# Exponentials on VectorE in int16, four tiles at once, and background matmuls as column tiles

## The chip, the core and the metric

The kernel runs on one core of a Trainium2 chip, as one launch. The metric is the device time of one execution in microseconds. Five engines work in parallel, each through its own queue of instructions in order: PE (TensorE, matmuls), ACT (ScalarE), DVE (VectorE), POOL (GpSimd) and SP, which here only issues DMAs. Matmuls write to PSUM, which here is eight banks of 128 x 512 fp32.

## The reference

One input x of 2048 rows and 512 columns (bf16) is normalised by rows, and the result goes through attention with 32 heads of 16 and through a gated feed-forward block; the output is x plus both.

```
xn = _layernorm(x)
# attention: q, k, v of 32 heads, 16 wide each
scores = jnp.einsum("bhqd,bhkd->bhqk", q, k) * (Dh ** -0.5)
p = _softmax(scores, axis=-1)
o = jnp.einsum("bhqk,bhkd->bhqd", p, v)
# feed-forward: F = 1792
gate = jnp.einsum("bsd,df->bsf", xn, W_gate);  up = jnp.einsum("bsd,df->bsf", xn, W_up)
h = gate * (gate > 0) * up
return x + o_as_rows @ wo + jnp.einsum("bsf,fd->bsd", h, W_down)
```

The softmax needs 32 x 2048 x 2048 exponentials. They are the bulk of the elementwise work.

## The kernel before

**Tiles of scores.** The heads stand eight to a group of 128 partitions (four groups, gg), two to each 32 partitions (ee is 0 or 1, j is 0 to 3). A tile is one head, 128 keys and 512 queries, so that there are 2048 tiles in the order c4 (512 queries), gg, ee, kt (128 keys), j. A score matmul contracts over 32 partitions, in which the other of the two heads is masked to zero; the mask is on k: `proj_k` writes two copies of kT, one for each ee (line 561), and `proj_q` one of qT (line 551; the first one on ACT, line 549). The four j use four row groups of the array (`tile_position=(32 * j, 0)`, line 796), and can run at the same time.

**Exponentials.** ACT takes the tiles in units of 3 and 2 in turn, out of two sets of score banks (ps_sc: three and two banks), and writes bf16 to a ring of 7 slots for each size (line 865). 208 tiles, spread evenly over tiles 96 to 2007, go to DVE in pairs (`dve_exp`): a score goes to bank 2 of ps_b (line 796), is scaled and clamped to a fixed-point int32 in dt_sb (line 810, d1), and when two are there, four more instructions of 1024 elements form the exponential of the pair: d2 (line 821), d3 (823), d4 (825) and d5 (828), the last writing the bf16 bit pattern as int16. They read the upper or lower half of each 32-bit word.

**P V.** For each kt, four matmuls (j = 0 to 3) with 17 columns of v_aug (16 of v and one of ones, for the row sum) stand on four column groups of the array and accumulate in bank 0 of ps_b over the 16 kt of a block (line 777). After each of the 32 blocks (c4, gg, ee), `normalise` copies the bank out (line 749), brings the sums through three DMAs and a reciprocal to all partitions, and POOL multiplies (line 764).

**Background.** The projections, the feed-forward block (`glu`: 56 pieces with eight matmuls, a copy of up, line 649, and a gate product, line 653, each; weights by two DMAs a piece) and the output rows (`out_rows`) run beside the attention. All of them go through `mm_chain` (line 537): full 128 x 128 matmuls in groups of two, with bank 1 of ps_b as the target, and a wanted place for each group among the units of ACT (`slots`; at most one group to a unit). Where a unit has no such work, the score group begins with a matmul on zeros (line 848), whose output the scores then overwrite.

**What sets the order.** Nothing is scheduled on the chip: the program builds a list of operations (`G.op`), each with an engine, a duration in ns as the writer puts it, a priority and the tiles that it reads and writes. `Graph.run` plays them through one by one, always placing the operation that can start first (by priority among those that are not late), and so fixes each engine's order. Pools with a fixed number of slots (ring, ps_b, ps_sc, ws, hT and so on) add waits for a slot's last users. `emit` then puts in the semaphore waits. So a change of any duration or priority can reorder everything.

Of the kernel before, what the change touches and what calls it, by code (L numbers as in the profile page):

```python
# [28 lines left out]
NRING = 7  # L29
PV_LAG = 7.0  # L30
NWS = 3
NDR = 3
ND_TILES = 210
D_FIRST = 96
D_LAST = 2048 - 40
# [3 lines left out]
C_K = 0.07802452  # L39
C_C = 1.83833913  # L40
C_A = 1.05904682
C_B = 6.97125146
FX = 65536.0
NUP = 1
NHT = 1
# [20 lines left out]
class Op:  # L66
    __slots__ = ("eng", "dur", "fn", "deps", "order", "prio", "acq", "name", "idx", "start", "end",
                 "done", "left", "users", "signal", "sem", "val", "waits", "stream", "lat", "seq", "hb", "after")


class Graph:
# [4 lines left out]
    LAT = {"PE": 150.0, "ACT": 220.0, "DVE": 100.0, "POOL": 120.0, "SP": 0.0}  # L76

    def __init__(self):
        self.ops = []
        self.units = {}  # L80

    def op(self, eng, dur, fn, reads=(), writes=(), prio=0.0, order=(), name="", stream=None, lat=None, after=None):
        o = Op()
        o.eng, o.dur, o.fn, o.prio, o.name = eng, dur, fn, prio, name
# [11 lines left out]
        for t in writes:  # L96
            if t.pool is not None and not t.w:
                o.acq.append(t)
            for w in t.w:
                if w.eng == eng and eng == "PE":  # L100
                    o.order.add(w)
                else:
                    o.deps[w] = True
            for r in t.r:
                if r.eng == eng and eng in ("PE", "ACT"):
                    o.order.add(r)
                else:
                    o.deps[r] = True
        for t in reads:
            t.r.append(o)  # L110
# [7 lines left out]
    def run(self):  # L118
# [33 lines left out]
        def earliest(o):  # L152
# [5 lines left out]
            for t in o.acq:  # L158
                b = slot_for(t)
                if b is None:  # L160
                    return None
                at = max(at, b[0])
            return at

        while n < len(ops):
            best = None
            for e in self.ENGS:
                pick = None
                for o in cand[e]:
                    at = earliest(o)  # L170
                    if at is None:
                        continue
                    at = max(at, free[e])
                    late = at > free[e] + 1e-6
                    key = (late, at if late else 0.0, o.prio, o.idx)
                    if pick is None or key < pick[0]:
                        pick = (key, at, o)
                if pick is not None and (best is None or pick[1] < best[0]):
                    best = (pick[1], e, pick[2])
# [4 lines left out]
            for t in o.acq:  # L184
                i = slot_for(t)[1]
# [14 lines left out]
            free[e] = at + o.dur  # L200
# [6 lines left out]
        self.span = max(o.end for o in ops)  # L207

# [102 lines left out]
def bass_parallel_sum__mha_block__glu_gated_reglu__prompt_kernel(  # L311
# [14 lines left out]
    with ExitStack() as es:  # L326
# [23 lines left out]
        kT = sb("kT", [128, 8, S], BF16)  # L350
        qT = sb("qT", [128, 4, 512], BF16)
        v_aug = sb("v_aug", [128, NT, H, VW], BF16)
        ring = sb("ring", [128, NRING * 5, 512], BF16)
        dt_sb = sb("dt_sb", [128, 2, 2 * 512], I32)
        dq_sb = sb("dq_sb", [128, 2 * 512], FP32)
        dw_sb = sb("dw_sb", [128, 2 * 512], BF16)
        dring = sb("dring", [128, NDR, 2 * 512], BF16)
        hT = sb("hT", [128, NHT * FT, 512], BF16)
# [14 lines left out]
        P_dt, P_dv, P_dq, P_dw, P_dr = (Pool(n, k) for n, k in (("dt", 2), ("dv", 1), ("dq", 1), ("dw", 1), ("dr", NDR)))  # L373
# [4 lines left out]
        P_h = Pool("h", NHT)  # L378
# [15 lines left out]
        G.op("DVE", 100, lambda e: e.tensor_scalar(hmask[:, 1:2], pid[:, 0:1], 1.0 / 16.0, None, op0=ALU.mult),  # L394
             reads=[t_pid], writes=[t_mask], prio=-889)
        G.op("DVE", 100, lambda e: e.tensor_scalar(hmask[:, 0:1], pid[:, 0:1], -1.0 / 16.0, 1.0, op0=ALU.mult, op1=ALU.add),
# [63 lines left out]
        def ln_block(b, pr):  # L460
# [11 lines left out]
            for i in range(4):  # L472
                m = 4 * b + i
                t_st, t_mv = Tile(), Tile()
                G.op("DVE", 640, lambda e, m=m: e.bn_stats(stats[:, m, :], xs(m)), reads=[t_xm[m]], writes=[t_st], prio=pr)
                G.op("DVE", 130, lambda e, m=m: e.bn_aggr(mv[:, m, :], stats[:, m, :]), reads=[t_st], writes=[t_mv], prio=pr - 0.1)
# [8 lines left out]
            for i in range(4):  # L485
                m = 4 * b + i
                t_n = Tile("xn", P_xn)
                G.op("DVE", 360, lambda e, m=m, t=t_n: e.tensor_scalar(  # L488
# [5 lines left out]
                elif i % 2 == 0:  # L494
                    tp = Tile("tp", P_b, [0, 1, 2] if b < 3 else [1, 2])
# [19 lines left out]
                elif half == 1:  # L515
# [4 lines left out]
                    o = G.op("DVE", 690, ev, reads=[tp], writes=[Tile()], prio=pr + 0.1)  # L520
# [3 lines left out]
        t_q, t_k, t_v = {}, {}, {}  # L524
# [4 lines left out]
        def mm_chain(tile, pairs, reads, prio, per=2, sub=0, slots=None, dur=220):  # L529

            n = len(pairs)
            for k, a in enumerate(range(0, n, per)):
                def fn(e, a=a):
                    ins = None
                    for i in range(a, min(a + per, n)):
                        l, r = pairs[i]
                        ins = e.matmul(bank_of(tile, sub), l(), r(), start=(i == 0), stop=(i == n - 1))  # L537
                    return ins
                G.op("PE", dur * (min(a + per, n) - a) + 100, fn, reads=reads, writes=[tile],
                     prio=prio if prio < 0 else slots[k] if slots else prio, after=slots[k] if slots else None)  # L540

        def proj_q(c4, gg, prio=0.0, tile=None, sub=0, eng="DVE", slots=None):
# [4 lines left out]
            tq = t_q[(c4, gg)] = Tile("q", P_q)  # L547
            if eng == "ACT":
                G.op("ACT", 600, lambda e: e.activation(qT[:, tq.slot, :], bank_of(t, sub), ACTF.Copy), reads=[t], writes=[tq], prio=prio)
            else:  # L550
                G.op("DVE", 690, lambda e: e.tensor_copy(qT[:, tq.slot, :], bank_of(t, sub)), reads=[t], writes=[tq], prio=prio)

        def proj_k(gg, b, prio=0.0, tile=None, sub=0, slots=None, gap=0.02):
            t = tile or Tile("pk", P_b, [0, 1, 2] if (gg, b) in ((0, 1), (0, 2)) else [1, 2] if gg == 0 else [1])
# [3 lines left out]
            dsts = [kT[:, 2 * gg + ee, 512 * b:512 * b + 512] for ee in range(2)]  # L558
            for ee in range(2):
                tk = t_k[(gg, ee, b)] = Tile("k")  # L560
                G.op("DVE", 690, lambda e, ee=ee: e.tensor_scalar(dsts[ee], bank_of(t, sub), hmask[:, ee:ee + 1], None, op0=ALU.mult),
                     reads=[t, t_masks[ee]], writes=[tk], prio=prio + gap * ee)

        def proj_v(kt, prio, allowed=(1,)):
            t = Tile("pv", P_b, list(allowed))
            mm_chain(t, [((lambda dt=dt: xnT[:, dt, 128 * kt:128 * kt + 128]), (lambda dt=dt: Wv[:, dt, :]))
                         for dt in range(DT)], [t_wv, t_xnT[kt // 4]], prio, slots=[1.3 * kt] * 2)
            tv = t_v[kt] = Tile("v")
            G.op("DVE", 690, lambda e: e.tensor_copy(v_aug[:, kt, :, 0:DH], bank_of(t).rearrange("p (h d) -> p h d", h=H)),  # L569
                 reads=[t], writes=[tv], prio=prio)  # L570
# [4 lines left out]
        on_dve, acc = set(), 0.0  # L575
        for i in range(D_FIRST, D_LAST):
            acc += ND_TILES / (D_LAST - D_FIRST)
            if acc >= 1.0:
                acc -= 1.0
                on_dve.add(i)  # L580
        if len(on_dve) % 2:
            on_dve.discard(max(on_dve))
        units, starts, at_unit, cur = [], [], [], []
        for i, t in enumerate(tiles):
# [4 lines left out]
            if len(cur) == SIZES[len(units) % 2] or i == len(tiles) - 1:  # L589
                units.append(cur)  # L590
                cur = []
        NU = len(units)
# [22 lines left out]
        for kt in range(NT):  # L615
            proj_v(kt, -684 + 10 * (kt // 4) + 0.1 * kt, allowed=(0, 1, 2) if kt < 8 else (1, 2))


        guard = Tile("wv")
        guard.r.extend(t_wv.w + t_wv.r)  # L620
        P_dv.cur[0] = guard
# [12 lines left out]
        def glu(c4, ft, slots):  # L634
            if c4 not in t_h:
# [275 lines left out]
```

## Time and profile before

| | us |
|---|---|
| time, median of 3 runs (904.47 to 912.19) | 908.67 |
| span of the profiled execution, first to last instruction | 901.3 |
| its own time beside the span | not given |
| PE busy, 5328 matmuls | 794.2 |
| DVE busy, 947 instructions | 741.8 |
| ACT busy, 743 instructions | 845.9 |
| POOL busy, 56 instructions | 62.7 |
| mean granted PE clock | 0.976 |

A page of the profile gives each engine's busy time, and busy time counts an instruction from its start to the end of its pipeline, so neighbours overlap; what one instruction costs its engine is the distance from its start to the next start. "Idle before" is put down to the instruction that ended the wait. Line numbers are those of this kernel.

### The profile page before, as it was taken

What the parts mean: (1) busy time and instruction counts of PE and PEld (TensorE: products, weight loads), DVE (VectorE), ACT (ScalarE), POOL (GpSimd) and SP (SyncE); (2) the same over time, 40 slices, a digit from 0 to 9 for tenths busy, and PEclk for the clock granted to TensorE, in tenths of its full rate; (3) what the DMA queues carried; (4) which work ended last, traced back from release to release, by engine and by line L of the source; (5) the groups of instructions that cost most, each with busy time, mean ns of one, the idle gap of its engine ahead of it and who ended that gap; (6) DMA issues with size and microseconds to landing.
All of it is one profiled execution on the core that took longest, in us unless ns stands there. A gap on an engine that the chain in (4) does not pass through costs nothing.

```text
span 901.3 us, 13005 instructions
## 1 busy us (share of the span) xinstructions
PE 794.2 (88%) x5328; PEld 220.4 (24%) x5427; DVE 741.8 (82%) x947; ACT 845.9 (94%) x743; POOL 62.7 (7%) x56
## 2 busy tenths in 40 slices
PE   7898898888889998888889999888888999999982
PEld 2322222222222222222222222222222222222220
DVE  8858899999985989979894899989997599999221
ACT  4699999999989999999999999999999999999992
POOL 3200000000000010000000001000000000000000
PEclk9999999999979999999999999999999999999996
DMA  5311111110001121111000011111100122220001
GB/s 172 98 25 37 36 36 37 36 31 19 2 25 36 32 60 35 26 42 48 13 25 25 24 43 48 43 48 24 25 13 25 36 54 60 59 51 16 25 13 36
DMA packets 84091, 34.66 MB, mean 38 GB/s; under 512 B 69952, under 2 KB 79936, under 8 KB 84032
## 3 DMA queue, kind: packets, MB, share of 16 engines
q1 hardware_dynamic: 84032, 33.83, 14.2%
q8 instruction: 42, 0.69, 0.3%
q14 instruction: 17, 0.14, 0.0%
HBM read 31.20 MB, written 2.36 MB: 37 GB/s over the span
## 4 chain that ended last, share of the span: by engine, by line
ACT 56%; PE 30%; DVE 8%; DMA 2%; issue 1%; POOL 0%; SPq 0%; POOLq 0%; ACTq 0%
ACT ring L865 56%; PE ps_b L537 11%; PE ps_sc L796 9%; PE ps_b L777 5%; PE ps_sc L848 3%; PE ps_b L796 2%; DVE dq_sb L823 2%; DMA rb<-rec_scr 1%; DVE dt_sb L810 1%; DVE Wv L821 1%; DVE xn_sb L488 1%; DVE dw_sb L825 1%; DMA x_sb<-in_A_x_dram 1%; DVE dring L828 1%; DVE v_aug L569 0%
## 5 line engine op out<-in xcount | busy, mean ns | idle before, releaser
L865 ACT ACTIVATE ring<-ps_sc 128x1536 bf16<-128x1536 f32 x736 | 841.5, 1270 | 29.0 <-PE ps_sc L796 26.8
L796 PE MATMUL ps_sc<-qT,kT 32*128 32x512 bf16 x1840 | 291.8, 388 | 43.9 <-ACT ring L865 36.2
L777 PE MATMUL ps_b<-ring,v_aug 128*17 128x512 bf16 x1840 | 192.4, 385 | 3.5 <-DVE o_sb L749 1.5
L810 DVE TENSOR_SCALAR dt_sb<-ps_b 128x512 int32<-128x512 f32 x208 | 142.1, 683 | 20.9 <-PE ps_b L796 16.1
L828 DVE SCALAR_TENSOR_TENSOR dring<-dt_sb,dw_sb 128x1024 int16<-128x1024 int16 x104 | 129.3, 1243 | 9.5 <-PE ps_b L777 9.3
L796 PEld LDWEIGHTS ps_sc<-qT,kT 32*128 32x128 bf16 x1840 | 70.3, 91 | 258.5 <-ACT ring L865 163.9
L823 DVE SCALAR_TENSOR_TENSOR dq_sb<-dt_sb 128x1024 f32<-128x1024 uint16 x104 | 130.6, 1255 | 0.0
L825 DVE SCALAR_TENSOR_TENSOR dw_sb<-dq_sb,Wv 128x1024 bf16<-128x1024 f32 x104 | 128.9, 1239 | 0.3
L848 PE MATMUL ps_sc<-zeros 128*128 128x512 bf16 x235 | 90.9, 387 | 17.7 <-ACT ring L865 16.8
L764 POOL TENSOR_TENSOR x_sb<-o_sb,rb 128x512 bf16<-128x512 f32 x28 | 43.1, 1540 | 695.6 <-DMA rb<-rec_scr 628.7
L796 PE MATMUL ps_b<-qT,kT 32*128 32x512 bf16 x208 | 80.3, 386 | 3.2 <-DVE dt_sb L810 1.8
L777 PE MATMUL ps_b<-dring,v_aug 128*17 128x512 bf16 x208 | 80.1, 385 | 0.0
L777 PEld LDWEIGHTS ps_b<-ring,v_aug 128*17 128x17 bf16 x1840 | 45.4, 88 | 126.2 <-issue 118.1
L821 DVE TENSOR_SCALAR Wv<-dt_sb 128x1024 f32<-128x1024 uint16 x104 | 72.2, 694 | 1.5
L537 PE MATMUL ps_b<-Wd,hT 128*128 128x512 bf16 x209 | 65.8, 402 | 3.9 <-issue 2.6
L537 PE MATMUL ps_b<-xnT,wgs 128*128 128x512 bf16 x216 | 61.5, 383 | 4.2 <-DVE up_sb L649 2.8
L537 PE MATMUL ps_b<-xnT,wus 128*128 128x512 bf16 x197 | 61.1, 390 | 4.4 <-issue 4.1
L653 DVE SCALAR_TENSOR_TENSOR hT<-ps_b,up_sb 128x512 bf16<-128x512 f32 x56 | 38.4, 686 | 12.8 <-PE ps_b L537 12.3
L848 PEld LDWEIGHTS ps_sc<-zeros 128*128 128x128 bf16 x261 | 25.1, 96 | 86.5 <-ACT ring L865 70.9
L649 DVE COPY up_sb<-ps_b 128x512 f32<-128x512 f32 x56 | 38.3, 684 | 5.1 <-PE ps_b L537 4.8
L749 DVE COPY o_sb<-ps_b 128x512 f32<-128x512 f32 x32 | 22.0, 688 | 15.8 <-PE ps_b L777 15.7
L537 PE MATMUL ps_b<-Wo_p,x_sb 128*128 128x512 bf16 x101 | 31.9, 386 | 1.6 <-issue 1.1
(60 smaller groups left out, 300.5 us busy)
## 6 DMA issues: line engine op xcount, KB each, us to landing
rb<-rec_scr SPq DMA_DIRECT2D x32, 256.0 KB
wus<-in_B_W_up_dram SPq DMA_DIRECT2D x56, 128.0 KB, 2.5
wgs<-in_B_W_gate_dram SPq DMA_DIRECT2D x56, 128.0 KB, 2.3
xr_sb<-in_A_x_dram SPq DMA_DIRECT2D x16, 128.0 KB, 4.1
out_dram<-xn_sb SPq DMA_DIRECT2D x16, 128.0 KB, 1.7
Wd<-in_B_W_down_dram SPq DMA_DIRECT2D x1, 1792.0 KB, 8.5
x_sb<-in_A_x_dram SPq DMA_DIRECT2D x3, 512.0 KB, 4.2
Wv<-in_A_wqkv_dram SPq DMA_DIRECT2D x1, 512.0 KB, 6.0
```

The source lines that it names most:

```text
L537: ins = e.matmul(bank_of(tile, sub), l(), r(), start=(i == 0), stop=(i == n - 1))
L653: G.op("DVE", 690, lambda e: e.scalar_tensor_tensor(out=hT[:, FT * th.slot + ft, :], in0=bank_of(tg), scalar=0.0, in1=up_sb[:, tup.slot, : ...
L764: G.op("POOL", 1200, lambda e: e.tensor_tensor(oT_of(tn), o_sb[:, to.slot, :], rb[:, trb.slot, :], ALU.mult), reads=[to, trb], writes=[tn] ...
L777: ins = e.matmul(ps_b[32 * j:32 * j + VN, 0, :], v_aug[:, kt, 8 * gg + 2 * j + ee, 0:VN], src[j][1](), start=(kt == 0), stop=(kt == NT - 1 ...
L796: return e.matmul(bank, kT[32 * j:32 * j + 32, 2 * gg + ee, 128 * kt:128 * kt + 128], qT[32 * j:32 * j + 32, t_q[(c4, gg)].slot, :], start ...
L810: G.op("DVE", 700, lambda e: e.tensor_scalar(dt_sb[:, td.slot, 512 * i:512 * i + 512], ps_b[:, 2, :], 0.25 * LOG2E * FX, -127.0 * FX, op0= ...
L821: G.op("DVE", 600, lambda e: e.tensor_scalar(Wv[:, :, :].rearrange("p a b -> p (a b)").bitcast(FP32), half(0), C_C * FX, C_K / FX ** 3, op ...
L823: G.op("DVE", 1140, lambda e: e.scalar_tensor_tensor(out=dq_sb[:], in0=half(0), scalar=C_A * FX, in1=half(0), op0=ALU.add, op1=ALU.mult), ...
L825: G.op("DVE", 1140, lambda e: e.scalar_tensor_tensor(out=dw_sb[:], in0=dq_sb[:], scalar=C_B * FX * FX, in1=Wv[:, :, :].rearrange("p a b -> ...
L828: G.op("DVE", 1140, lambda e: e.scalar_tensor_tensor(out=dring[:, tr.slot, :].bitcast(I16), in0=half(1), scalar=128.0, in1=dw_sb[:].bitcas ...
L848: e.matmul(ps_sc[:, 3 * k0, :], zeros[:, 0:128], zeros[:], start=True, stop=True)
L865: return e.activation(ring[:, a:a + n, :], ps_sc[:, 3 * k0:3 * k0 + n, :], ACTF.Exp, scale=0.25)
```

## The change

DVE takes 436 tiles and not 208: for each block (c4, gg, ee), the list QUADS says how many of its 16 kt go to DVE whole, with all four j (109 in all). The units of ACT hold the rest.

A quad (`quad`) is four score matmuls through the same bank 2 of ps_b, each followed by one DVE instruction that adds a constant, clamps at zero and writes int16 (d1); then three instructions over all 2048 elements: d2 keeps the lower seven bits and sets an exponent, d3 multiplies that, read as bf16, with the first number, read as bf16, and d4 keeps the exponent bits of the first number. The exponential is the sum of the two bf16 tensors, and is not formed: P V runs twice, once with each (`pv_stream`), and the row sums with it. Three quad buffers stand in place of the fixed-point ones.

The scale that turns a score into an exponent is put into q: `hmask` holds QSCALE and zero, `proj_q` writes two masked copies of qT, and `proj_k` one plain copy of kT. ACT's exp gets a scale to match.

`mm_chain` issues each 128 x 128 matmul as four matmuls of 32 columns on the four column groups, one such four to an operation and not two. Transposes stay as they were.

The planner knows three modes of the array (row tiles, column tiles, full) and charges a change between them; it may start a score on free row groups beside one that has just started; it marks ACT's scores as urgent; it puts a P V on zeros (17 columns, adding nothing) into P V's bank where PE has room, in place of the matmul on zeros before the scores. All durations are written anew. The feed-forward buffer has 20 slots of one piece (hT) and not one of 14, so that the next 512 rows can start before the last are read, and the pieces are spread evenly over the run. The ring has 6 slots of each size. The projections of k, q and v get other wanted places, and the evictions of q, k, v and of the feed-forward block higher priorities.

```diff
 SIZES = (3, 2)
-NRING = 7
+NRING = 6
-NDR = 3
-ND_TILES = 210
-D_FIRST = 96
-D_LAST = 2048 - 40
+NQD = 3
+LEAD = 9
+QUADS = [1] + [3, 4, 3] + [4, 3, 4, 3] * 7
+NHS = 20
...
-                        ins = e.matmul(bank_of(tile, sub), l(), r(), start=(i == 0), stop=(i == n - 1))
+                        w, x = l(), r()
+                        for j in range(4):
+                            ins = e.matmul(bank_of(tile, sub)[32 * j:32 * j + 32, :], w[:, 32 * j:32 * j + 32], x,
+                                           start=(i == 0), stop=(i == n - 1), tile_position=(0, 32 * j))
...
-                G.op("DVE", 690, lambda e: e.tensor_copy(qT[:, tq.slot, :], bank_of(t, sub)), reads=[t], writes=[tq], prio=prio)
+                    G.op("DVE", 655, lambda e, ee=ee: e.tensor_scalar(qT[:, tq.slot, ee, :], bank_of(t, sub), hmask[:, ee:ee + 1], None, op0=ALU.mult),
...
-                G.op("DVE", 690, lambda e, ee=ee: e.tensor_scalar(dsts[ee], bank_of(t, sub), hmask[:, ee:ee + 1], None, op0=ALU.mult),
+            G.op("DVE", 601, lambda e: e.tensor_copy(kT[:, gg, 512 * b:512 * b + 512], bank_of(t, sub)), reads=[t], writes=[tk], prio=min(prio, -600))
...
+        def quad(key, kt, u):
+            c4, gg, ee = key
+            tq = Tile("qd", P_qd)
+            ti, tu = Tile("qi"), Tile("qu")
+            for n, j in enumerate(range(4)):
+                ts = Tile("ds", P_b, [2])
+                t = key + (kt, j)
+                o = G.op("PE", 213, lambda e, t=t: score(e, ps_b[:, 2, :], t), reads=[t_q[key], t_k[(gg, kt // 4)]], writes=[ts],
+                         prio=u - 50, name="dsc", mode="row", rows=[j], after=u - LEAD)
+                G.op("DVE", 601, lambda e, j=j: e.tensor_scalar(qd[:, tq.slot, 0, 512 * j:512 * j + 512], ps_b[:, 2, :], IBIAS, 0.0,
+                                                                op0=ALU.add, op1=ALU.max), reads=[ts], joins=[tq], prio=-500, name="d1")
+                ti.w.append(G.ops[-1])
...
+            G.op("DVE", 600, lambda e: e.tensor_scalar(xu(), xi(), 0x7F, 0x3F00, op0=ALU.bitwise_and, op1=ALU.bitwise_or),
+                 reads=[ti], writes=[tu], prio=u, name="d2")
+            o = G.op("DVE", 1133, lambda e: e.tensor_tensor(xu().bitcast(BF16), xi().bitcast(BF16), xu().bitcast(BF16), ALU.mult),
+                     reads=[ti], writes=[tu], prio=u, name="d3")
...
+            G.op("DVE", 600, lambda e: e.tensor_scalar(xi(), xi(), 0x7F80, 0x0001, op0=ALU.bitwise_and, op1=ALU.bitwise_or),
+                 reads=[ti], writes=[te], prio=u, name="d4")
+            for half, tr in ((1, tu), (0, te)):
+                pv_stream(key, kt, [(lambda j=j, half=half: qd[:, tq.slot, half, 512 * j:512 * j + 512].bitcast(BF16)) for j in range(4)],
+                          [tr, tq], u, u + PV_LAG)
...
-            def sc(e, cl=cl, k0=k0, idle=u > 24 and u not in busy):
+            def sc(e, cl=cl, k0=k0):
                 ins = None
-                if idle:
-
-                    e.matmul(ps_sc[:, 3 * k0, :], zeros[:, 0:128], zeros[:], start=True, stop=True)
...
+        def blank(e):
+            ins = None
+            for j in range(4):
+                ins = e.matmul(ps_b[32 * j:32 * j + VN, 0, :], zeros[:, 0:VN], zeros[:], start=False, stop=False, tile_position=(0, 32 * j))
+            return ins
+        G.filler = (P_b, blank)
```

## Prediction

> **What bounds the kernel now.** I read the page's busy shares first, then the groups by shape, the stages, the longest pieces of the chain of waits, and stretches of the timeline for the real cost of one instruction.
>
> ```profile
> PE 794.2 (88%) x5328; PEld 220.4 (24%) x5427; DVE 741.8 (82%) x947; ACT 845.9 (94%) x743; POOL 62.7 (7%) x56
> ```
>
> ACT is busy for 845.9 us of 901.3 and nearly all of it is the 736 exps of line 865. The stages (us of the stage, then busy us and count of PE, PEld, DVE, ACT, POOL, the granted PE clock, DMA share, GB/s) say where it is not:
>
> ```profile
> 0.00:30.00 30.00, 24.27 (x134) 9.37 (x136) 25.73 (x59) 18.04 (x19) 8.59 (x21) 0.94 0.60 181
> 30.00:60.00 30.00, 26.68 (x182) 8.53 (x185) 22.97 (x35) 21.07 (x19) 4.73 (x3) 0.94 0.06 21
> 100.00:200.00 100.00, 88.23 (x605) 24.92 (x618) 96.22 (x121) 98.35 (x87) 4.58 (x4) 1.00 0.12 29
> 500.00:600.00 100.00, 92.00 (x617) 24.56 (x627) 93.84 (x116) 97.84 (x86) 6.08 (x3) 0.97 0.15 37
> 860.00:901.00 41.00, 21.94 (x138) 5.71 (x138) 7.08 (x11) 23.43 (x21) 2.53 (x2) 0.80 0.08 27
> ```
>
> From 100 us on ACT is full to within 2 or 3%; it loses 21 us in the first 60 us (the first exp starts at 15.9) and 17.6 us behind the last exp. The chain of waits has one unbroken piece that prices an exp: 75.04/66 = 1.137 us for the mean of a 3-tile and a 2-tile exp.
>
> ```profile
> 686.84 75.04 ACT ring L865 x66
> ```
>
> Who waits for whom:
>
> ```profile
> PEld ps_sc L796 <- ACT ring L865: 163.9, 357, 1.2
> ACT ring L865 <- PE ps_sc L796: 26.8, 43, 3.6
> ```
>
> PE waits for ACT to free score banks far oftener than ACT waits for scores. So ACT is the bound; PE and DVE have slack.
>
> Busy PE and DVE are counted with pipeline ends, so I price them from start to start. PE:
>
> ```profile
> 505.45 1.04 PE L537 MATMUL ps_b<-Wd,hT 128*128 128x512 bf16 x4
> 506.42 0.40 PE L777 MATMUL ps_b<-ring,v_aug 128*17 128x512 bf16 x4
> 506.75 0.39 PE L796 MATMUL ps_sc<-qT,kT 32*128 32x512 bf16 x3
> 507.07 0.61 PE L537 MATMUL ps_b<-Wo_p,x_sb 128*128 128x512 bf16 x2
> ```
>
> Three scores on different row groups cost 0.32 us (506.75 to 507.07), a P V group of four column tiles 0.33, four full matmuls 0.97: that is 0.213 to 0.216 for each slot of the array and 0.107 for a change between row tiles, column tiles and the full array. DVE:
>
> ```profile
> 26.89 1.37 DVE L488 TENSOR_SCALAR xn_sb<-x_sb,mv,rstd 128x512 bf16<-128x512 bf16 x4
> 28.18 0.68 DVE L569 CAST v_aug<-ps_b 128x512 bf16<-128x512 f32 x1
> 28.81 0.69 DVE L519 COPY xnT<-ps_b 128x1024 bf16<-128x1024 bf16 x1
> 29.42 0.68 DVE L569 CAST v_aug<-ps_b 128x512 bf16<-128x512 f32 x1
> 32.02 1.38 DVE L561 TENSOR_SCALAR kT<-ps_b,hmask 128x512 bf16<-128x512 f32 x2
> 33.32 0.17 DVE L476 BATCH_NORM_AGGREGATE mv<-stats 128x2 f32<-128x6 f32 x1
> 86.09 0.69 DVE L810 TENSOR_SCALAR dt_sb<-ps_b 128x512 int32<-128x512 f32 x1
> 86.69 1.22 DVE L828 SCALAR_TENSOR_TENSOR dring<-dt_sb,dw_sb 128x1024 int16<-128x1024 int16 x1
> 87.83 0.25 DVE L757 RECIPROCAL rrec<-rsum 128x16 f32<-128x16 f32 x1
> ```
>
> 512 elements from PSUM take 0.60 (86.09 to 86.69), 1024 unpacked ones 1.13 (86.69 to 87.83): 1.035 ns an element and 0.07 fixed. 1024 packed bf16 take 0.61 (28.81 to 29.42): two elements a step. A per-partition mask costs 0.05 more (1.30/2 = 0.65, line 561). The four of line 488 take 1.29, 0.32 each; less 0.07 and two pointers at 0.05 that is 0.15 for 512, between three and four elements a step.
>
> **The change, part by part.**
>
> *ACT.* Tiles on DVE go from 208 to 436 (109 quads of four by the list QUADS), so exps from 736 to 645: 91 x 1.137 = 103.5 us off the engine that bounds. 901.3 - 103.5 = 797.8 if every idle stretch stays as it is. The second ACT copy of q in the prologue, at the 0.60 of the present one (line 549), stands ahead of the first exp: +0.6. The exp's other scale costs nothing.
>
> *DVE.* It loses the old chain, 208 x 0.60 + 104 x (0.60 + 3 x 1.13) = 541. It gains 436 first steps at 0.60 (262) and per quad two bitwise steps and a product of 2048 elements. Bitwise: 0.60 at four a step, 1.13 at two; I take 0.60, since line 488 is the only 16-bit SBUF-to-SBUF row and it lies nearer four. The product reads two packed tensors; no row has that. Its ends are 0.60 and the 2.19 of an unpacked element (line 828's rate); I take 1.13, two a step, because packing gave line 519 two on one input and a second input costs nothing in the 0.60 of the other evictions. Quad: 4 x 0.60 + 2.33 = 4.74; 109 of them 516. K evictions fall from 32 x 0.65 to 16 x 0.60 (-11), q's go from 15 x 0.60 to 30 x 0.65 (+10). The rest (up, hT, O, v, layernorm, sums) stays at about 135. Sum: 706 before, 681 after. Of 764 us between the first exp and the last (797.8 less 16 and 17.6) that is 89%, against 81% now: it still lies beside ACT, but with half the cover.
>
> The Trainium skill ("VectorE: DVE Perf Modes", the perf-mode tier table) gives a 16-bit tensor_scalar from SBUF the 4x mode and tensor_tensor 2x at most; by it the DVE sum is the same 681, and no run here has shown either on int16.
>
> *PE.* Counted along its order of instructions, before and after: slots of the array for the background 992 and 992 (now four 32-column tiles each), P V 512 and 621 (1612/4 = 403 for the tiles of ACT, two for each of 109 quads), idle fillers 261 full ones and 69 column ones; scores 1840 + 208 and 1612 + 436; changes of mode 1803 and 1291. Row time rises from 190 to 199 (same-row neighbours run one behind the other), column time from 111 to 363, full-array time falls from 278 to 7, changes from 193 to 138. Sum: 771 before, 707 after, 93% of 764 where it was 89% of 868. But 56 us of the old sum were fillers with their switches on top, and only 15 of the new are: the part that can't yield rises from about 78% to 90%. That a column tile 32 wide costs what one 17 wide does is not in the trace; its ends are 0.216 a group (506.42) and four times that, and I take 0.216, since these rows differ only in width.
>
> ```profile
> 311.31 0.61 PE L777 MATMUL ps_b<-ring,v_aug 128*17 128x512 bf16 x8
> 312.28 0.39 PE L796 MATMUL ps_sc<-qT,kT 32*128 32x512 bf16 x3
> ```
>
> Sixteen column tiles (four groups, this row and its neighbours) take 0.97 with a switch, again 0.216 a group.
>
> The Trainium skill ("TensorE: Matmul & The Clock Gate", Part 3, measured speedup) speaks against this change: it has 2.38x for three column tiles and 3.07x for four row tiles. By 3.07 a group would cost 0.281, 1682 groups 110 us more, and PE would need 817 us and end the run near 858. The row says 0.216, and the row decides here.
>
> *Waits that are added.* The four scores of a quad pass through one bank (ps_b 2), each behind the DVE step before it. PE is in order, so a late DVE step holds the score of the next exp behind it, and ACT waits. DVE queues up the same way behind its 32 reciprocals, which wait for a DMA (11.3 us in all now, 1.9 at most) and are covered today by 19% of DVE idle. Against it: background work now goes in pieces of 0.216 and not 0.432, so less stands ahead of a due score. ACT's losses between 100 and 860 us are 16 us now. Below, they vanish (-16). Above, PE keeps today's idle share of 11%: 707/0.89 = 794 where ACT alone would take 764 (+30). I take +10, nearer the present rows than either end.
>
> *The rest.* DMAs are the same in number and size; the order of weights among the 32 normalisation chains on SP shifts, and these chains are late-insensitive (POOL stands idle 629 us for them). POOL's instructions are unchanged. The feed-forward block's hT buffer of 20 tiles lets its pieces be spread evenly; the P V ring holds 12 exps and not 14, 13.6 us of ACT, and costs nothing while P V runs less than that behind; if PE falls back further, ACT waits and the PE rival below holds. The tail of 17.6 is the last normalisation chain and stays.
>
> Sum: 797.8 + 0.6 + 10 = 808.4 of span. The page gives no time of this execution beside its span; I add the difference between span and median, 908.67 - 901.3 = 7.4 (the fastest run would make it 3.2). Predicted 815.8, say 816.
>
> **Rivals.** *PE becomes the bound.* For it: 93% of the stretch, and a stall of DVE reaches PE at once. Against it: PE waited 164 us for ACT in its loads alone. From 708 us of PE at today's idle share: 764 -> 794, which ends at 836; with clock dips (0.94 to 0.97 in the stages above) at 850.
>
> *One DVE step is slower than taken.* Bitwise at two a step adds 109 x 2 x 0.53 = 116, the product unpacked adds 109 x 1.06 = 116: DVE 797, which with 16.5 ahead, 17.6 behind and 7.4 makes 838, and 855 with some idle.
>
> *Slower than before.* All three 2048-element steps run unpacked, as every int16 row of the present chain does (line 828). Place: DVE; price: 3 x 2.19 = 6.57 instead of 2.33 a quad, DVE 681 + 462 = 1143, time about 1184. It decides from the point where DVE fills the present time: (867 - 164 - 262)/109 = 4.05 us for the three steps. Against it: line 828's source steps over every second 16-bit word, the new ones are contiguous, like line 488.
>
> *It is all hidden.* Waits shrink with the small pieces and nothing is added: 790 to 799.
>
> **How the numbers follow.** Forecast (own range 800 to 832) 0.63; all hidden 0.12; PE bound 0.12; one slow DVE step 0.07; all slow 0.06. The range 789 to 855 leaves out the last and the fringes. A difference of under 1% can't be told from none here. Faster by over 1%: 0.92; within 1%: 0.02; slower: 0.06.
>
> **What would show it.** Right: 645 exps with unbroken pieces at 1.137; d2 and d4 at 0.60 start to start, d3 at 1.13; ACT's idle between 100 us and the last exp under 35 us; ACT busy at 93%, DVE near 90%. Wrong: start to start of d3 at 2.19 or of d2 at 1.13; four column tiles of the background at more than 0.22; ACT waiting for ps_sc by over 60 us; a granted clock under 0.95 in the middle stages.

## The result and the profile after

The changed kernel takes 797.18 us (median of five runs, 796.42 to 804.70) where the kernel before took 908.67: the ratio is 0.8795, 95% interval 0.8751 to 0.8839. The forecast of 816 had the sign and the range right and is 19 us too high. The execution that was profiled is the slowest of the five: 804.7 us, of which 802.9 are its span. The four others have spans of 794.6 to 796.2, and in every run of this kernel 1.8 us lie around the span.

First the busy shares on the page of the kernel after, and the costliest groups (busy us, mean ns of one, then the idle time before them and what ended it):

```profile
PE 753.1 (94%) x8854; PEld 224.8 (28%) x8854; DVE 717.0 (89%) x1085; ACT 738.0 (92%) x653; POOL 56.5 (7%) x56
...
L965 ACT ACTIVATE ring<-ps_sc 128x1536 bf16<-128x1536 f32 (+1 forms) x645 | 732.9, 1347 | 36.2 <-PE ps_b L883 17.6
L913 DVE TENSOR_SCALAR qd<-ps_b 128x512 int16<-128x512 f32 x436 | 298.3, 684 | 51.1 <-PE ps_b L900 42.4
...
L924 DVE TENSOR_TENSOR qd<-qd 128x2048 bf16<-128x2048 bf16 x109 | 135.4, 1242 | 0.4
...
L922 DVE TENSOR_SCALAR qd<-qd 128x2048 int16<-128x2048 int16 x109 | 78.9, 724 | 2.2
```

ACT has 645 exps and not 736. It is still the fullest by cost, but PE and DVE now stand beside it, and the largest part of the idle time before the exps, 17.6 of 36.2 us in 8 waits, is ended by line 883, P V: the exp had its scores and waited for a slot of the ring. Before the change it was the scores that came last.

The stages of the kernel after (columns as in the prediction):

```profile
100.00:200.00 100.00, 97.93 (x1208) 29.01 (x1200) 97.38 (x148) 100.00 (x90) 5.10 (x4) 1.00 0.20 48
...
500.00:600.00 100.00, 95.17 (x1074) 26.86 (x1070) 95.15 (x144) 97.92 (x87) 5.08 (x4) 0.96 0.18 45
600.00:700.00 100.00, 97.48 (x1126) 28.35 (x1119) 87.50 (x127) 93.98 (x83) 6.55 (x4) 0.94 0.15 37
```

From 100 to 200 us ACT has no idle time at all, although PE and DVE are both busy for over 97 of the 100. Behind the first 100 us, the largest loss in one place lies where the granted clock fell, at half clock from 591 to 611 us of this execution.

```profile
585.00:591.00 6.00, 5.63 (x60) 1.49 (x52) 5.49 (x9) 6.00 (x7) 0.00 (x0) 1.00 0.00 0
591.00:611.00 20.00, 19.08 (x130) 3.49 (x131) 14.79 (x21) 16.17 (x14) 2.30 (x1) 0.52 0.09 28
```

In those 20 us PE finished 130 matmuls where it finishes about 240 at full clock, and ACT stood idle for 3.8, of 18.0 us ahead of its exps from 100 us to the last one. The chain of waits prices an exp again, 171.00/151 = 1.1325 us:

```profile
271.71 171.00 ACT ring L965 x151
```

VectorE's timeline shows the new steps one behind the other (start us, duration with the end of the pipeline):

```profile
210.92 0.69 DVE L913 TENSOR_SCALAR qd<-ps_b 128x512 int16<-128x512 f32 x1
211.52 1.22 DVE L924 TENSOR_TENSOR qd<-qd 128x2048 bf16<-128x2048 bf16 x1
212.65 0.69 DVE L913 TENSOR_SCALAR qd<-ps_b 128x512 int16<-128x512 f32 x1
213.25 0.69 DVE L928 TENSOR_SCALAR qd<-qd 128x2048 int16<-128x2048 int16 x1
213.85 0.69 DVE L740 COPY up_sb<-ps_b 128x512 f32<-128x512 f32 x1
```

From start to start d1 takes 0.60, d3 1.13 and d4 0.60; d2 takes 0.61 elsewhere (208.32 to 208.93).

### The profile page after: what moved, and what is told of

It is laid out like the page before. It is cut to its first block, busy times and chain, and to the rows that moved or that the text cites. A ratio compares the mean times of both kernels' runs of the same rounds, so it can differ in the third digit from the quotient of the medians.

```text
span 802.9 us, 19989 instructions
## 1 busy us (share of the span) xinstructions
PE 753.1 (94%) x8854; PEld 224.8 (28%) x8854; DVE 717.0 (89%) x1085; ACT 738.0 (92%) x653; POOL 56.5 (7%) x56
## 3 DMA queue, kind: packets, MB, share of 16 engines
q8 instruction: 69, 1.13, 0.6%
## 4 chain that ended last, share of the span: by engine, by line
ACT 61%; PE 22%; DVE 11%; DMA 4%; issue 1%; POOL 1%; SPq 0%; POOLq 0%; DVEq 0%
ACT ring L965 61%; PE ps_b L628 8%; PE ps_sc L900 5%; PE ps_b L883 4%; DVE qd L913 3%; PE ps_b L900 3%; DVE qd L924 2%; DMA rb<-rec_scr 2%; DVE qd L922 2%; DMA x_sb<-in_A_x_dram 1%; DVE qd L928 1%; DVE xn_sb L577 1%; PE ps_b L990 1%; DMA rec_scr<-rrec 1%; DVE xn_sb L779 0%
## 5 line engine op out<-in xcount | busy, mean ns | idle before, releaser
L965 ACT ACTIVATE ring<-ps_sc 128x1536 bf16<-128x1536 f32 (+1 forms) x645 | 732.9, 1347 | 36.2 <-PE ps_b L883 17.6
L913 DVE TENSOR_SCALAR qd<-ps_b 128x512 int16<-128x512 f32 x436 | 298.3, 684 | 51.1 <-PE ps_b L900 42.4
L900 PE MATMUL ps_sc<-qT,kT 32*128 32x512 bf16 x1612 | 260.4, 390 | 11.8 <-ACT ring L965 9.1
L900 PE MATMUL ps_b<-qT,kT 32*128 32x512 bf16 x436 | 169.0, 388 | 6.4 <-DVE qd L913 6.0
L883 PE MATMUL ps_b<-ring,v_aug 128*17 128x512 bf16 x1612 | 143.5, 385 | 2.5 <-DVE o_sb L851 1.7
L924 DVE TENSOR_TENSOR qd<-qd 128x2048 bf16<-128x2048 bf16 x109 | 135.4, 1242 | 0.4
L900 PEld LDWEIGHTS ps_sc<-qT,kT 32*128 32x128 bf16 x1612 | 61.6, 91 | 226.9 <-ACT ring L965 165.0
L883 PE MATMUL ps_b<-qd,v_aug 128*17 128x512 bf16 x872 | 82.0, 386 | 0.5 <-DVE qd L924 0.4
L922 DVE TENSOR_SCALAR qd<-qd 128x2048 int16<-128x2048 int16 x109 | 78.9, 724 | 2.2
L928 DVE TENSOR_SCALAR qd<-qd 128x2048 int16<-128x2048 int16 x109 | 77.5, 711 | 0.1
L628 PE MATMUL ps_b<-Wd,hT 128*32 128x512 bf16 x896 | 70.2, 394 | 1.9 <-POOL x_sb L866 1.0
L628 PE MATMUL ps_b<-xnT,wgs 128*32 128x512 bf16 x896 | 70.3, 384 | 0.8 <-DVE up_sb L740 0.5
L628 PE MATMUL ps_b<-xnT,wus 128*32 128x512 bf16 x896 | 68.7, 384 | 1.3 <-DVE hT L744 0.8
L900 PEld LDWEIGHTS ps_b<-qT,kT 32*128 32x128 bf16 x436 | 39.6, 91 | 68.6 <-DVE qd L913 61.1
L628 PEld LDWEIGHTS ps_b<-Wd,hT 128*32 128x32 bf16 x896 | 17.7, 96 | 35.1 <-issue 23.6
L628 PEld LDWEIGHTS ps_b<-xnT,wgs 128*32 128x32 bf16 x896 | 17.9, 94 | 32.6 <-issue 17.8
```

The costliest lines, as they stand in the source:

```text
L628: ins = e.matmul(bank_of(tile, sub)[32 * j:32 * j + 32, :], w[:, 32 * j:32 * j + 32], x, start=(i == 0), stop=(i == n - 1), tile_position= ...
L883: ins = e.matmul(ps_b[32 * j:32 * j + VN, 0, :], v_aug[:, kt, 8 * gg + 2 * j + ee, 0:VN], src[j](), start=(st[0] == 0), stop=(st[0] == st[ ...
L900: return e.matmul(bank, kT[32 * j:32 * j + 32, gg, 128 * kt:128 * kt + 128], qT[32 * j:32 * j + 32, q_slot[(c4, gg)].slot, ee, :], start=T ...
L913: G.op("DVE", 601, lambda e, j=j: e.tensor_scalar(qd[:, tq.slot, 0, 512 * j:512 * j + 512], ps_b[:, 2, :], IBIAS, 0.0, op0=ALU.add, op1=AL ...
L922: G.op("DVE", 600, lambda e: e.tensor_scalar(xu(), xi(), 0x7F, 0x3F00, op0=ALU.bitwise_and, op1=ALU.bitwise_or), reads=[ti], writes=[tu], ...
L924: o = G.op("DVE", 1133, lambda e: e.tensor_tensor(xu().bitcast(BF16), xi().bitcast(BF16), xu().bitcast(BF16), ALU.mult), reads=[ti], write ...
```

## The experiments

All edits are to the kernel after unless the text says otherwise. Times are medians; the ratio is to the kernel before, with its 95% interval.

**Fewer quads: is it the exps?** The same kernel with 52 quads, so that ACT has 736 exps as before. The planner puts 459 idle fillers (P V on zeros, four matmuls each) into the order of this run, where the kernel after has 69.

```diff
-QUADS = [1] + [3, 4, 3] + [4, 3, 4, 3] * 7
+QUADS = [1, 1, 2, 2, 2, 1, 2, 1, 2, 1, 2, 2, 1, 2, 1, 2, 1, 2, 2, 1, 2, 1, 2, 1, 2, 2, 1, 2, 2, 2, 2, 2]
```

> The changed kernel with 52 quads and not 109, so 208 tiles on VectorE and 736 exps on ScalarE, as before the change; all else as changed. Theory (the gain is the 91 exps taken from ScalarE, the rest of the change only makes room for it): 797 + 91 x 1.133 = 900 us, 890 to 904. Rival (column tiles, fewer changes of array mode and the new planner bring a good part of the gain themselves): 840 to 880 us.

Measured: 883.36 us, ratio 0.9746 (0.9696 to 0.9796), between the two. So 25 of the 111 us do not come from fewer exps, and 91 fewer bring 86.2 and not 103. The group of exps shows how ACT came by the 25:

```profile
L965 ACT ACTIVATE ring<-ps_sc 128x1536 bf16<-128x1536 f32 x736 | 833.5, 1401 | 16.5 <-PE ps_sc L900 9.6 <-PE ps_b L883 6.3 <-PE ps_b L900 0.3
```

From the first exp to the last the kernel before takes 866.7 us for 735 steps of 1.133, so 34 are lost; this one takes 847.1 and loses 14.

**Is it the lighter VectorE?** The same 52 quads, each with four more VectorE products into a buffer that nobody reads, which brings VectorE's load up again.

```diff
...
+            for n in range(4):
+                G.op("DVE", 1133, lambda e, n=n: e.scalar_tensor_tensor(out=junk[:, 2 * (n % 2):2 * (n % 2) + 2, :].rearrange("p a b -> p (a b)"),
...
+                     reads=[tu, tq], writes=[t_junk[n % 2]], prio=u, name="d6")
```

> The 52 quads kernel (883.4 us) with four more VectorE instructions of 1.13 us for each quad, whose output nobody reads: 235 us more, so that VectorE is about as busy as in the kernel before (742). Theory (of the 25 us that the 52 quads kernel is faster than before, VectorE's lighter load brings the most): 895 to 908 us. Rival (planner, column tiles and fillers bring them): 880 to 888 us.

Measured: 887.65 us, ratio 0.9796 (0.9746 to 0.9845). Of the 25 us about 20 stay with VectorE busy for 689 us instead of 458: its slack is not what brings most of them. (In the kernel before it is busy for 742, so that the old load is not quite reached.)

**Are they the column tiles?** The kernel before with column tiles for the background, and nothing else changed.

```diff
-                        ins = e.matmul(bank_of(tile, sub), l(), r(), start=(i == 0), stop=(i == n - 1))
+                        w, x = l(), r()
+                        for j in range(4):
+                            ins = e.matmul(bank_of(tile, sub)[32 * j:32 * j + 32, :], w[:, 32 * j:32 * j + 32], x,
+                                           start=(i == 0), stop=(i == n - 1), tile_position=(0, 32 * j))
```

> The kernel before the change with its background matmuls as four column tiles each, nothing else changed but the order that the planner makes of it: 1695 changes of mode, not 1803. Theory (ScalarE bounds, PE's saving of 12 us is hidden): 900 to 911 us. Rival (the column tiles bring part of the gain by themselves): under 890 us. If four column tiles cost more than one full matmul, the groups on PE show it: more than 0.22 us from one to the next.

Measured: 909.55 us, ratio 1.0042 (1.0002 to 1.0082). Alone they bring nothing: ACT bounds, and what happens on PE is hidden. The other way round, the kernel after with full background matmuls:

```diff
-                        w, x = l(), r()
-                        for j in range(4):
-                            ins = e.matmul(bank_of(tile, sub)[32 * j:32 * j + 32, :], w[:, 32 * j:32 * j + 32], x,
-                                           start=(i == 0), stop=(i == n - 1), tile_position=(0, 32 * j))
+                        ins = e.matmul(bank_of(tile, sub), l(), r(), start=(i == 0), stop=(i == n - 1))
...
-                     prio=prio if prio < 0 else at if slots else prio, after=at, mode="col")
+                     prio=prio if prio < 0 else at if slots else prio, after=at, mode="full")
```

> The changed kernel with each background matmul as one 128 x 128 matmul and not four column tiles; the planner is told so. PE's order then has 1555 changes of mode and not 1291 (28 us at 0.107) and 36 idle fillers, not 69 (7 us less). Theory (ScalarE bounds, PE is nearly full beside it): 802 to 818 us. Rival A (PE has room, all is hidden): 794 to 800 us. Rival B (the column tiles are what lets PE keep up): over 830 us.

Measured: 817.49 us, ratio 0.9016 (0.8962 to 0.9069): 20.3 us for about 20 us more of PE time by the planner's prices (264 changes of mode more at 0.107, 33 fillers less at 0.216). At 109 quads, work on PE is no longer hidden.

**The planner's charge for a change of mode.** It is told that a change costs nothing, and so makes 1555 of them and not 1291. It also finds room, as it believes, for 285 idle fillers and not 69.

```diff
-    SWITCH = 107.0
+    SWITCH = 0.0
```

> The changed kernel with the planner's price of a change of array mode at zero, so that it mixes row and column tiles freely: 1555 changes and not 1291 (28 us), and 285 idle fillers and not 69 (47 us) that it believes to fit. Theory (PE nearly full): 820 to 860 us. Rival (PE has room): 795 to 805 us.

Measured: 855.99 us, ratio 0.9442 (0.9383 to 0.9500). Waits of ACT for scores come back:

```profile
ACT ring L965 <- PE ps_sc L900: 47.6, 125, 1.4
```

There are 125 of them and the longest is 1.4 us: PE is a little late again and again, at a clock of 0.986. By the prices above PE has 75 us more to do, 28 for the changes and 47 for the fillers, and the time rises by 58.8; the run does not tell the two apart.

**The idle fillers.** No P V on zeros any more.

```diff
-        G.filler = (P_b, blank)
```

> The changed kernel without the 69 P V groups on zeros that the planner puts into idle time of PE. Theory (they fill gaps that nothing else uses, and hold the granted clock up a little): 797 to 806 us, clock 0.96 to 0.98. Rival A (they cost PE time that is wanted): 785 to 794 us. Rival B (without them the clock falls often): over 815 us, clock under 0.94.

Measured: 814.94 us, ratio 0.8988 (0.8927 to 0.9049), above what the theory gave. The stage from 100 to 760 us, after first, then without fillers:

```profile
100.00:760.00 660.00, 639.32 (x7525) 188.57 (x7521) 615.18 (x912) 642.43 (x567) 38.09 (x28) 0.98 0.16 39
```

```profile
100.00:760.00 660.00, 632.20 (x7201) 181.99 (x7197) 607.01 (x900) 636.30 (x560) 38.14 (x28) 0.95 0.16 39
```

PE has 276 matmuls less to do in all, and the granted clock falls from 0.98 to 0.95: 61 us in mid-run at half clock, not 20.5. Everything else on PE, VectorE and ScalarE stands in the same order in both runs. In the profiled executions (814.1 and 802.9 us) ScalarE is idle for 15 us in and just behind the stretches at half clock without the fillers, and for 5 with them, which is most of the difference. 69 fillers of four matmuls, which compute nothing, are worth 17.8 us.

**More quads.** If ACT alone bounds, each quad more takes 1.6 exps or 1.81 us off.

```diff
-QUADS = [1] + [3, 4, 3] + [4, 3, 4, 3] * 7
+QUADS = [1] + [4] * 31
```

> The changed kernel with 125 quads (500 tiles on VectorE, 619 exps). ScalarE loses another 26 x 1.133 = 29 us, VectorE gains 16 x 4.74 = 76 us, so 757 us of VectorE. Theory (three engines are nearly full, the next to bound is VectorE): 800 to 820 us, with VectorE over 93% of the span. Rival (ScalarE still bounds alone): 766 to 775 us.

Measured: 872.04 us, ratio 0.9610 (0.9539 to 0.9690). Both expectations missed by over 50 us. Eight quads more than 109:

```diff
-QUADS = [1] + [3, 4, 3] + [4, 3, 4, 3] * 7
+QUADS = [1] + [4, 3, 4] + [4, 3, 4, 4] * 7
```

> The changed kernel with 117 quads (468 tiles, 632 exps): ScalarE 15 us less, VectorE 38 us more (719). Theory (balance point near 109): 792 to 802 us. Rival (ScalarE still bounds alone): 781 to 785 us.

Measured: 836.00 us, ratio 0.9222 (0.9159 to 0.9286); both missed again. Four fewer than 109:

```diff
-QUADS = [1] + [3, 4, 3] + [4, 3, 4, 3] * 7
+QUADS = [1] + [3, 4, 3] * 10 + [4]
```

> The changed kernel with 105 quads (420 tiles, 651 exps). Theory (at 109 quads VectorE with its one score bank has taken over as the bound: from 109 to 117 and 125 a quad cost 4.9 and 4.5 us; below, ScalarE bounds and a quad is worth 1.81): the line from 52 quads gives 883.4 - 53 x 1.81 = 787 us, so 784 to 792. Rival (at 109 ScalarE still bounds): 797 + 4 x 1.81 = 804 us, 801 to 806.

Measured: 797.65 us, ratio 0.8810 (0.8780 to 0.8840), the time of 109 quads, and neither expectation. Side by side:

| quads | time, us | us for each quad more | ACT's waits for a ring slot |
|---|---|---|---|
| 52 | 883.4 | | 6.3 |
| 105 | 797.7 | -1.62 | 11.2 |
| 109 | 797.2 | -0.1 | 17.6 |
| 117 | 836.0 | +4.9 | 56.2 |
| 125 | 872.0 | +4.5 | 108.1 |

Between 52 and 105 a quad is worth 1.62 us on the mean, somewhat under ACT's price of 1.81, and no number in between was run, so that the gain may fade before 105. Above 109 a quad costs about what VectorE pays for it (4.74). ACT's and VectorE's waits with 117 quads (us in total, times, longest us):

```profile
PEld ps_b L900 <- DVE qd L913: 72.1, 213, 1.1
ACT ring L965 <- PE ps_b L883: 56.2, 24, 7.5
DVE qd L913 <- PE ps_b L900: 37.2, 61, 3.5
PEld ps_b L883 <- DVE qd L924: 21.2, 54, 1.4
```

and the same with 125:

```profile
ACT ring L965 <- PE ps_b L883: 108.1, 42, 9.0
```

The largest of these waits is that of a quad's score for the d1 ahead of it (72.1 us), three times that of a quad's P V for d3 (21.2). How it reaches ACT can be read from the longest wait for a slot with 117 quads, 7.5 us up to 776.16. PE in the last 5 us of it, and the exp:

```profile
771.08 0.39 PE L900 MATMUL ps_b<-qT,kT 32*128 32x512 bf16 x1
771.40 1.05 PE L628 MATMUL ps_b<-Wd,hT 128*32 128x512 bf16 x16
772.38 0.39 PE L900 MATMUL ps_b<-qT,kT 32*128 32x512 bf16 x1
772.69 1.05 PE L628 MATMUL ps_b<-Wd,hT 128*32 128x512 bf16 x16
773.67 0.39 PE L900 MATMUL ps_b<-qT,kT 32*128 32x512 bf16 x1
...
775.40 0.38 PE L900 MATMUL ps_b<-qT,kT 32*128 32x512 bf16 x1
775.71 0.83 PE L883 MATMUL ps_b<-ring,v_aug 128*17 128x512 bf16 x12
776.16 2.37 ACT L965 ACTIVATE ring<-ps_sc 128x1536 bf16<-128x1536 f32 x2 [7.51 <-PE ps_b L883]
```

The P V of ACT's tiles (775.71) stands in PE's fixed order behind scores of quads (L900 into ps_b), which come 1.3 to 1.7 us apart because each waits for VectorE, and behind the background that the planner put between them. The ring stays full meanwhile, and the exp waits. Over all 24 such waits 31 scores of quads and 77 background groups go ahead; where a block ends, P V also waits for VectorE to copy its bank out. With 125 quads the longest wait is 9.0 us. VectorE is 90% and 91% busy in these two, never full.

**A quad that costs more.** One more 0.60 us step on VectorE for each quad, whose result is not read.

```diff
...
+            G.op("DVE", 600, lambda e: e.tensor_scalar(junk[:], xu(), 0x7F, 0x3F00, op0=ALU.bitwise_and, op1=ALU.bitwise_or),
+                 reads=[tu, tq], prio=u, name="d6")
```

> The changed kernel with one more VectorE instruction of 0.60 us for each quad, whose output nobody reads: 65 us more on VectorE (746), nothing else. Theory (VectorE stands at 89% and has little left): 810 to 840 us. Rival (VectorE lies wholly beside ScalarE): 795 to 800 us.

Measured: 827.31 us, ratio 0.9135 (0.9070 to 0.9199): 30 of 65 us of added work show. VectorE is then 93% busy, so the 90% above is no hard limit of its own.

**Is it the length of the ring?** Seven slots of each size and not six.

```diff
-NRING = 6
+NRING = 7
```

> The changed kernel with a P V ring of 7 slots of each size and not 6. Theory (the longest waits of ScalarE, 17.6 us in 8 waits, are for a ring slot that P V holds while it waits for a quad, so that a longer ring bridges part of them): 786 to 793 us. Rival (VectorE's rate sets the pace, and a longer ring only moves the wait): 795 to 799 us.

Measured: 795.51 us, ratio 0.8787 (0.8754 to 0.8819), which can't be told from the kernel after. ACT's waits for a slot go from 17.6 to 13.4 us. 10.3 of these 13.4 us lie before 75 us. That a longer ring only fills later, where VectorE and PE are behind on the mean, would fit this and is not shown.

**Is it the one bank that a quad's scores pass through?** 117 quads with two such banks; since PSUM has eight in all, ACT's units shrink to 2 and 2 tiles, and the ring and the leads are set to match.

```diff
-SIZES = (3, 2)
+SIZES = (2, 2)
...
-                ts = Tile("ds", P_b, [2])
+                ts = Tile("ds", P_b, [2, 3])
```

> The 117 quads kernel (836.0 us) with units of 2 and 2 tiles on ScalarE in place of 3 and 2, which frees a PSUM bank: the scores of the quads take turns in two banks, not one (790 exps of 2 at 0.905 = 715 us, as 632 at 1.133; a P V ring of 32 tiles, not 30; P V lag and lead of a quad longer by a unit or two; PE has 1579 changes of mode, not 1301, 30 us, and 110 fillers less, 24 us). Theory (VectorE can't get over about 90% of its own cost because each score waits for the one bank): VectorE's wait for PE falls under 20 us from 37, and the time to 795 to 818 us. Rival (what paces VectorE is not the bank, but its own instructions or the P V behind it): 830 to 850 us.

Measured: 845.18 us, ratio 0.9336 (0.9288 to 0.9384). The time is not the one that the theory gave. The waits of VectorE and ACT:

```profile
DVE qd L913 <- PE ps_b L900: 6.4, 15, 1.3
DVE qd L913 <- PE ps_b L883: 30.3, 18, 10.4
ACT ring L965 <- PE ps_b L883: 47.3, 34, 6.2
ACT ring L965 <- PE ps_sc L900: 25.2, 25, 3.4
```

VectorE's wait for a score went as meant, from 37.2 to 6.4 us, and came back as a wait for P V to free a quad buffer, with PE at 95%. The run is no clean test of the bank, since PE also has 278 changes of mode more than with 117 quads and one bank. (The smaller units also make ACT's work dearer: 737.9 us busy instead of 725.7, for the same tiles.)

## Why the prediction was right, and where its sizes were off

**The exps: right in size, in part by luck.** The span of the profiled execution splits into 901.3 - 91 x 1.133 (103.1) + 2.7 (ACT's loss between first and last exp, 36.6 instead of 33.9) + 1.6 (first exp) + 0.5 (tail) = 803.0, against 802.9 measured. The loss is what is left over between the two exps, so the sum has to come out; what it tells is the size of each part. It hides two changes that nearly cancel. The prediction took "every idle stretch stays as it is". In fact the loss was 14 and not 34 with 52 quads, so the rest of the change removed 20 us of it, and with 109 quads about as much is back. That the two are alike was not foreseen and is luck.

Not all that is back comes from the added quads. ACT's idle time ahead of its exps, from 100 us to the last one, is 16.4 us before, 2.2 with 52 quads, 7.3 with 105 and 18.0 with 109, but about 5 of these 18.0 lie at the half clock near 600 us, and ring7, with 109 quads and no half clock in mid-run, has 6.9. Of the 17.6 us of waits for a ring slot 9.7 lie before 75 us, where the projections run; with 52 quads all 6.3 lie there.

What removed the 20 us is settled only in part. Column tiles put into the kernel before bring nothing (before_columns), and VectorE's slack brings about 5 of the 25, as far as its old load was restored (quads52_ballast). Another part goes with the clock: over 36 executions of the kernel before, span and mean granted clock have a correlation of -0.95 and a slope of 7.1 us for each 0.01 (896.6 us at 0.984, 912.9 at 0.962), and quads52 ran at 0.989 where the median one ran at 0.973. By that slope 11 us would be the clock. That is a correlation and no test, and the 459 idle fillers of quads52, which may be what holds its clock up, were not tried apart; nor were the new order, the finer pieces and the scores on free rows.

**VectorE: right.** d1 0.60, d2 0.61, d3 1.13, d4 0.60, as taken. Both ends for d3 (0.60 and 2.19) and 1.13 for the bitwise steps are out, and with them the rivals "one step is slower" and "slower than before". In the Trainium skill ("VectorE: DVE Perf Modes", the perf-mode tier table) 16-bit tensor_scalar has the 4x mode and tensor_tensor 2x at most; these rows agree, on int16 and with bitwise operations too.

**PE: right in price, and one rival nearly so.** Twelve column tiles 32 wide, in three groups, take 0.83 us with the end of the pipeline, and four take 0.40 (kernel after, 204.61 and 205.91 us):

```profile
204.61 0.83 PE L628 MATMUL ps_b<-xnT,wgs 128*32 128x512 bf16 x12
...
205.91 0.40 PE L628 MATMUL ps_b<-xnT,wgs 128*32 128x512 bf16 x4
```

(0.83 - 0.40)/2 = 0.215 a group, against the 0.216 taken. The 0.281 by the packing speedup in the Trainium skill ("TensorE: Matmul & The Clock Gate", Part 3, measured speedup) is not what a stream of groups costs here. "PE becomes the bound" did not happen at 109 quads, but full_background shows that it stood right there: 20 us more of PE cost 20 us.

**The waits that are added: mis-sized, and not where they were looked for.** The +10 was measured as +2.7 in the profiled execution, with 1.133 as the price of an exp on both sides. By the idle time in the two pages' rows of exps (29.0 and 36.2 us) it is 7.2; the price makes part of the difference, since an exp of the kernel before takes 1.137. Little of it lies in mid-run, where ACT's idle time goes from 16.4 to 18.0 us behind the first 100. The mechanism named, a score of a quad held up by VectorE and the next exp held up behind it, is there (61.1 us of weight loads wait for d1), but it costs ACT little directly: only 3.8 us of its idle time is ended by a quad's score. What it does is delay P V, which stands behind those scores, and half of ACT's idle time is the wait for a ring slot. The sentence on the ring ("costs nothing while P V runs less than that behind") names the right condition. That it fails with eight more quads, where the time is 836, was not seen. One sign of being wrong that the prediction named did come: the clock is 0.94 from 600 to 700 us.

**The second copy of q and the start.** +0.6 was taken; the first exp starts 1.6 later (17.5 instead of 15.9), and the first piece of the chain, the load of x, ends 1.6 later (6.59 us instead of 5.04). The copy itself adds nothing that can be seen.

**Around the span: wrong.** The 7.4 that was added was not time around the span. That is 1.8 here. The rest was the distance between a quick execution of the kernel before, which had been profiled, and its median. Part of that goes with the clock: by the slope above, 0.976 against a median of 0.973 is 2 of the 5.6 us. Of the 18.6 us between 815.8 and 797.2, 5.6 are this term, 5.5 the too high span (808.4 instead of 802.9), and 7.5 that the profiled execution, with its half-clock stretch, is slower than the median one.

**What stays open.** Why the knee lies near 109, and why VectorE gets no further than 90 to 94% of its own cost. By cost, a block with four quads needs 4 x 4.74 + 5.2 = 24.1 us of VectorE and 48/2.5 x 1.133 = 21.8 of ACT; with three it is 19.4 and 23.6. So three and four in turn is where the two meet, and more fours must lose. But the loss is larger than this: with 125 quads VectorE's steps add up to 681 + 16 x 4.74 = 757 us, and the stretch that they had, the span of 871 less 35 at both ends, is 836. VectorE's own rate, PE at 93 to 95% and the quad buffers between them may hold each other up; two_banks117 showed only that freeing one moves the wait to the next. More quad buffers, or 117 quads with less work on PE, were not tried. Nor was the mask tried on k instead of q by itself.

## What to carry to other kernels

When work is moved off the engine that bounds, count what it loads onto the next two engines in the stretch that matters. The gain for each piece can turn into a loss at the next engine's full price before that engine is full: here a quad brought 1.6 us on the mean up to 105 of them and cost 4.9 beyond 109, with VectorE's busy share at 88% (105 quads) and 90% (117). Test the split on both sides of the choice, and run the change with the old split too, since part of a gain may come from what went in beside it. Once three engines are nearly full, work on any of them may cost its own length, and a small edit that was free before, like full matmuls in place of tiles, no longer is.

## What the runs showed of the hardware

- Matmuls on zeros can make a kernel faster: 276 of them, 25 us of busy time, are worth 17.8 us. Without them, and with the rest of the order on PE, VectorE and ScalarE the same, the granted clock is at half for 61 us of mid-run instead of 20.5.
- The clock also fell where PE had been busy: 5.63 of the 6 us ahead of the 20 us at half clock. What set it off is not in the trace.
- A large VectorE step and a POOL multiply hold each other up. In the kernel after, first where VectorE started ahead, then where POOL did:

```profile
600.13 1.22 DVE L924 TENSOR_TENSOR qd<-qd 128x2048 bf16<-128x2048 bf16 x1
600.18 2.30 POOL L866 TENSOR_TENSOR x_sb<-o_sb,rb 128x512 bf16<-128x512 f32 x1 [15.51 <-DMA rb<-rec_scr]
...
661.96 1.27 POOL L866 TENSOR_TENSOR x_sb<-o_sb,rb 128x512 bf16<-128x512 f32 x1 [26.25 <-DMA rb<-rec_scr]
662.03 2.27 DVE L924 TENSOR_TENSOR qd<-qd 128x2048 bf16<-128x2048 bf16 x1
664.23 0.68 DVE L913 TENSOR_SCALAR qd<-ps_b 128x512 int16<-128x512 f32 x1
```

At 600.18 the multiply takes 2.30 us instead of its median of 1.27; at 662.03 d3 takes 2.20 us from start to start instead of 1.13. All 16 steps d2, d3 and d4 that took over 0.1 us longer than usual overlap a POOL multiply. The Trainium skill ("SBUF — State Buffer", SBUF: two separate sides) has an exclusive lock on a shared pair of ports for such a case, and these rows agree with it. Above their medians the means of d2, d3 and d4 add up to 109 x (0.031 + 0.026 + 0.028) = 9 us of VectorE, which the prediction left out.
